# Memory sums of half 0 in 64-row tiles, token sums behind pv(1), and the value copies dealt out anew between ScalarE and VectorE

## The chip, the cores and the metric

The kernel runs on one core of a Trainium2 chip. Its time is the device time of one execution, in microseconds (us); of several runs the median counts. The core's engines run side by side and hand work to each other by semaphores: TensorE (PE in the profile, its weight loads PEld), VectorE (DVE), ScalarE (ACT), GpSimd (POOL) and SyncE (SP), which issues DMAs. TensorE writes its products to PSUM, which is divided into banks; VectorE and ScalarE read them from there and write bfloat16 copies to SBUF, where TensorE can read them.

## The reference

Four stages follow each other, each adding its output to x: A, B, A, B. Stage A is attention over segments of 32 tokens with 8 memory rows that pass from one segment to the next, so the 64 segments of a stage run one after the other. Stage B is a gated mixer over all 2048 tokens; the change doesn't touch it.

```python
def _A_ref(x, mem0, Wq, Wk, Wv, Wo, seg_len):      # x (1, 2048, 512), mem0 (1, 8, 512), Wq/Wk/Wv (512, 32, 128)
    mask = (idx[:, None] < M) | (idx[:, None] >= idx[None, :])
    mem = mem0
    for s in range(n_seg):                          # 64 segments
        h = concatenate([mem, xs], axis=1)          # 8 + 32 rows
        q, k, v = einsum('btd,dhe->bhte', h, Wq), ..., ...
        scores = where(mask, einsum('bhqe,bhke->bhqk', q, k) * scale, -1e9)
        p = softmax(scores, axis=-1)
        o = einsum('bhqk,bhke->bhqe', p, v)
        o = einsum('bhte,hed->btd', o, Wo)
        mem = o[:, :M, :]
        outs.append(o[:, M:, :])
x = x + _A_ref(_layernorm(x), ...)
x = x + _B_ref(_layernorm(x), ...)
x = x + _A_ref(_layernorm(x), ...)
x = x + _B_ref(_layernorm(x), ...)
```

## The kernel before

`a_block` runs stage A and calls `segment` for each of the 64 segments, 128 in the two stages. The order of TensorE, VectorE and ScalarE is the order in which the source issues their instructions; each engine works off its own list in that order, and the semaphores between them are set by a layer that follows which tile each instruction reads and writes. Accesses of two engines to one PSUM bank are ordered too, unless the source declares that there is no dependency (`tc.declare_no_dep`).

The 32 heads go in two halves of 16, r = 0 and 1. One segment does, in TensorE's order:

- queries and keys, four chunks of 16 products of 512 columns (psQ, psm, psK; `mm_chunk`, line 753). TensorE works here as four column tiles of 32 columns each, so four products run together. ScalarE copies each chunk to rows (line 1078), VectorE transposes it (line 1081).
- `v_mm(0)`: the values of half 0, into psK[:, 1, :], with `scores(0)` (lines 1104 and 1108) among them. ScalarE takes the exponential of the scores into S (`exps`, line 1113), VectorE multiplies it by the mask into E (`close`, line 1116). VectorE copies the values to VA[:, 0] (line 1202).
- `v_mm(1)`: the values of half 1, into the bank psW (called psV in the profile), 16 products in four groups. `scores(1)` stands after the second group, `sums_zero` after the third, and the fourth group comes last. ScalarE copies the values to VA[:, 1] (line 1217).
- a piece of other work (`fill`): products for later blocks, psb or pwB in the profile, four of them at this place.
- `pv(0)`: probabilities times values of half 0 (lines 1153 and 1156). From here to `pv(1)` TensorE works as two row tiles of 64 rows and 128 columns each; the keys of one half lie in 128 partitions, and each 64 of them belong to other heads.
- `sums_tokens`: the softmax denominators of the 32 token queries, by products of E with a matrix of ones (line 1145), into psT; `sums_one`: those of the 8 memory queries of half 1 (line 1136), into free columns of psO[1]; `pv(1)`.
- another `fill`, then the output projection of the memory rows: `wo_pairs` for heads 0 to 15 (px, line 936), `wo_rest` for heads 16 to 31 (line 943). It reads uT, which VectorE makes from psO and Rm (`memory_out`, line 1174).

Rm is the inverse of a memory sum, by a logarithm (line 1170) and an exponential (line 1171) on ScalarE (`inverse`). The memory sums of half 0 are made by `sums_zero` in 32-column tiles: 16 products whose left side is `half`, a constant with ones in 64 of its 128 rows and zeros in the others, so that all 128 rows can be streamed and only one group's heads count (line 1127). They land in columns 224 to 352 of the first scores' bank, psS[:, 0, :].

Of the kernel before, what the change touches and what calls it, by code (L numbers as in the profile page):

```python
# [7 lines left out]
BF16 = mybir.dt.bfloat16  # L8
# [6 lines left out]
P = 128  # L15
# [51 lines left out]
def _consts(ctx, tc, c, b_sp, between):  # L67
    nc = tc.nc
    cp = ctx.enter_context(tc.tile_pool(name="consts", bufs=1))
    bsp = cp.tile([P, 16], F32, name="bsp")  # L70
    tctx = ExitStack()
    tmp = tctx.enter_context(tc.tile_pool(name="consts_tmp", bufs=1))
    maskf = tmp.tile([P, 224], F32, name="maskf")
    nc.gpsimd.memset(maskf[:], 1.0)
    fourth = tmp.tile([P, 4, 32], F32, name="fourth")
    nc.gpsimd.memset(fourth[:], 0.0)
    nc.gpsimd.affine_select(out=fourth[:], in_=fourth[:], compare_op=ALU.not_equal, fill=1.0,
                            base=0, pattern=[[-1, 4], [-4, 32]], channel_multiplier=1)
    own = maskf[:, 160:224].rearrange("p (i q) -> p i q", i=4)
    is_own = tmp.tile([P, 4, 1], F32, name="is_own")  # L80
    nc.vector.tensor_reduce(out=is_own[:], in_=fourth[:], op=ALU.max, axis=mybir.AxisListType.X)
    nc.vector.tensor_copy(own, is_own[:].to_broadcast([P, 4, 16]))
    between()
    for q in range(0, P, 32):
        blk = maskf[q:q + 32, 0:160].rearrange("p (i q) -> p i q", i=4)[:, :, 8:32]
        nc.gpsimd.affine_select(out=blk, in_=blk, compare_op=ALU.is_ge, fill=0.0, base=8,
                                pattern=[[0, 4], [1, 24]], channel_multiplier=-1)
        last = own[q:q + 32, :, 8:16]
        nc.gpsimd.affine_select(out=last, in_=last, compare_op=ALU.is_ge, fill=0.0, base=0,
                                pattern=[[1, 4], [4, 8]], channel_multiplier=-1)  # L90
    maskN = cp.tile([P, 2, 224], BF16, name="maskN")
    nc.vector.memset(maskN[:], 0.0)
    for gs in range(4):
        nc.vector.tensor_copy(maskN[32 * gs:32 * gs + 32, gs % 2, :], maskf[32 * gs:32 * gs + 32, :])
    ones = cp.tile([P, P], BF16, name="ones")
    nc.vector.memset(ones[:], 1.0)
    half = cp.tile([P, 2, 32], BF16, name="half")
    nc.vector.memset(half[:], 0.0)
    for g in range(2):
        nc.vector.memset(half[64 * g:64 * g + 64, g, :], 1.0)  # L100
    bsp_bf = cp.tile([P, 16], BF16, name="bsp_bf")

    def load_bsp():
        nc.vector.memset(bsp_bf[:], 0.0)
        nc.sync.dma_start(bsp_bf[:], b_sp.rearrange("(t p) -> p t", p=P))
        return lambda: nc.vector.tensor_copy(bsp[:], bsp_bf[:])

    c["bsp"], c["load_bsp"] = bsp, load_bsp
    tctx.close()
    c.update(maskN=maskN, ones=ones, half=half)  # L110
    return c


# [504 lines left out]
def cols_rhs(w, j, kt, cg):  # L618
    at = 2048 * (j % 2) + 512 * cg
    return w[j // 2][:, kt, at:at + 512]  # L620
# [88 lines left out]
def a_block(tc, c, rows, front, MV_in, RS_in, MV_out, RS_out, ahead, wo, S, first):  # L709
    nc = tc.nc  # L710
    NSEG = S // SEG
    NB = S // P
    scale = float(DH) ** -0.5
    maskN, ones, half = c["maskN"], c["ones"], c["half"]

    with ExitStack() as ctx:

# [33 lines left out]
        def mm_chunk(ps, lhs, rhs, kts=range(KT)):  # L751

            return [nc.tensor.matmul(ps[32 * cg:32 * cg + 32, :], lhsT=lhs(kt, cg), rhs=rhs(kt, cg), start=(kt == 0), stop=(kt == KT - 1),  # L753
                                     tile_position=(0, 32 * cg)) for kt in kts for cg in range(4)]

        def other_bank(mms, *reads):

            for m in mms:
                for r in reads:
                    tc.declare_no_dep(m.ins, r.ins, reason="another bank of the tile")  # L760
# [300 lines left out]
        def segment(s, fill, spare1, spare2, spare3, tail, loads):  # L1061
# [4 lines left out]
            VA = vsp.tile([P, 2, 4, DH], BF16, name="VA")  # L1066
# [6 lines left out]
            E = segp.tile([P, 2, 2, 224], BF16, name="E", bufs=1)  # L1073
# [9 lines left out]
            def v_mm(r, ps, kts=range(KT)):  # L1083
                return mm_chunk(ps, lambda kt, cg: hA_cur[:, kt, :], lambda kt, cg: cols_rhs(w, 4 + r, kt, cg), kts)

            def ends(q):

                return q.rearrange("p h (b e) -> p h b e", e=8)[:, :, 0:5:4, :]
# [5 lines left out]
            def heads40(q):  # L1094
                return q.rearrange("p (i q) -> p i q", q=40)
# [16 lines left out]
            def exps(r):  # L1112
                return nc.scalar.activation(out=S[:, r], in_=psS[:, r, 0:224], func=ACT.Exp, scale=scale)  # L1113

            def close(r):
                nc.vector.tensor_tensor(out=E[:, r], in0=S[:, r].unsqueeze(1).to_broadcast([P, 2, 224]), in1=maskN[:], op=ALU.mult)

            def e_all(e, lo, hi):

                return e[:, :, 0:160].rearrange("p n (i q) -> p n i q", q=40)[:, :, :, lo:hi]  # L1120

            def e_own(e, b):
                return e[:, :, 160:224].rearrange("p n (i b e) -> p n i b e", i=4, b=2)[:, :, :, b, :]

            def sums_zero(pN):

                return [nc.tensor.matmul(pN[32 * cg:32 * cg + 32, 64 * g:64 * g + 64], lhsT=half[:, g, :], rhs=e_own(E[:, 0], 0) if k else e_all(E[:, 0], 0, 8),
                                         start=False, stop=True, tile_position=(0, 32 * cg), skip_group_check=True)
                        for k in range(2) for g in range(2) for cg in range(4)]

            def sums_one():

                for k in range(2):
                    for g in range(2):
                        e = E[64 * g:64 * g + 64, 1]
                        nc.tensor.matmul(psO[1][:, g, 320:384], lhsT=ones[64 * g:64 * g + 64, :], rhs=e_own(e, 0) if k else e_all(e, 0, 8),
                                         start=(k == 0), stop=True, skip_group_check=True)

            def sums_tokens(ps):

# [7 lines left out]
            def pv(r):  # L1148

                for i in range(4):  # L1150
                    for g in range(2):
                        o = psO[r][:, g, 0:320].rearrange("p (s i q) -> p s i q", s=2, i=4)[:, :, i, :]
                        nc.tensor.matmul(o, lhsT=VA[64 * g:64 * g + 64, r, i, :], rhs=E[64 * g:64 * g + 64, r, :, 40 * i:40 * i + 40],  # L1153
                                         start=(r == 0 and i == 0), stop=True, skip_group_check=True)
                for g in range(2):
                    nc.tensor.matmul(ends(heads40(psO[r][:, g, 0:320])), lhsT=VX[64 * g:64 * g + 64, j4, r, :],
                                     rhs=E[64 * g:64 * g + 64, r, :, 160:224], start=False, stop=True, skip_group_check=True)
# [10 lines left out]
            def inverse(r, src):  # L1168
                rm = Rm[:, r]
                nc.scalar.activation(out=rm, in_=src, func=ACT.Ln)  # L1170
                return lambda: nc.scalar.activation(out=rm, in_=rm, func=ACT.Exp, scale=-1.0)  # L1171
# [19 lines left out]
            psK = attO[0].tile([P, 2, 512], F32, name="psK")  # L1191
# [4 lines left out]
            psS = att.tile([P, 2, 512], F32, name="psS")  # L1196
            scores(0)
            expd = exps(0)
            qk_T(3, r3)
            other_bank(v_mm(0, psK[:, 1, :], (1, 2, 3)), read)  # L1200
            close(0)
            nc.vector.tensor_copy(VA[:, 0].rearrange("p i e -> p (i e)"), psK[:, 1, :])
            if j4 == 0 and tb + 1 < NB and not begin:
                ln_turn(tb + 1)
            if begin:
# [1 line left out]
            psW = accB.tile([P, 512], F32, name="psV")  # L1207
            v_mm(1, psW, (0, 1))
            other_bank(scores(1), expd)
            expd = exps(1)  # L1210
            v_mm(1, psW, (2,))
            pN = psS[:, 0, 224:352]
            other_bank(sums_zero(pN), expd)
            v_mm(1, psW, (3,))
            Rm = segp.tile([P, 2, 2, 64], F32, name="Rm", bufs=1)
            invert = inverse(0, pN.rearrange("p (g q) -> p g q", g=2))
            nc.scalar.copy(VA[:, 1].rearrange("p i e -> p (i e)"), psW[:])
            invert()
            close(1)

            psO = [attO[r].tile([P, 2, 512], F32, name="psO") for r in range(2)]
            if not begin:
                fill()
            pv(0)
            psT = att.tile([P, 2, 512], F32, name="psT")
            sums_tokens(psT)
            sums_one()
            pv(1)
            memory_out(0)
            spare1(E)  # L1230
            if not begin:
# [62 lines left out]
        start = nc.vector if first else nc.gpsimd  # L1294
# [137 lines left out]
        for i in range(H // 2):  # L1432
            for k in range(4):
                h = 2 * i + k % 2
                nc.tensor.matmul(pw[32 * k:32 * k + 32, :], lhsT=ends[k // 2][:, h, :], rhs=wo.head(h).rearrange("p (kt g el) -> p g kt el", kt=4, g=4),
                                 start=(i == 0), stop=(i == H // 2 - 1), tile_position=(0, 32 * k))
# [46 lines left out]
```

## Time and profile before

| | |
|---|---|
| median of 3 runs | 1620.24 us |
| lowest and highest | 1613.57 and 1620.24 us |
| profiled execution, its own time | 1608.14 us |
| its span, first to last instruction | 1606.4 us |
| TensorE busy | 1574.8 us, 98% |
| VectorE busy | 1071.0 us, 67% |
| ScalarE busy | 1052.2 us, 65% |
| GpSimd busy | 305.7 us, 19% |

The page of the profile gives busy time and instructions of each engine, the span in 40 slices, the chain of work that ended last, and the costliest groups of instructions (line, engine, operation, output<-inputs, shapes, count | busy us, mean ns of one | idle time of the engine before them and who ended most of it). Other views list who waited for whom, the instructions in order of time, or the busy time in chosen stretches. A busy share is a mean over stages with different limits; what a change in one stage is worth is read from that stage.

### The profile page before, as it was taken

The numbers are of one execution on the slowest core, as the hardware profiler recorded it, in microseconds if no ns is written. First come the engines' busy times: TensorE is split into PE (matmuls) and PEld (weight loads), VectorE is DVE, ScalarE is ACT, GpSimd is POOL, SyncE is SP. The second block draws the span as 40 slices with busy tenths as digits, with TensorE's granted clock in tenths as the row PEclk, the third lists the DMA queues.
The fourth block names the chain that finished last, engine by engine and source line by source line (L and its number), as shares of the span: only waits on it lengthen the run. The fifth ranks groups of instructions, "written<-read, shape, count | busy, mean of one in ns | idle before, by whom it ended". The sixth has DMA issues, their size and how long they took to land.

```text
span 1606.4 us, 90912 instructions
## 1 busy us (share of the span) xinstructions
PE 1574.8 (98%) x41021; PEld 974.9 (61%) x41046; DVE 1071.0 (67%) x3066; ACT 1052.2 (65%) x2279; POOL 305.7 (19%) x674
## 2 busy tenths in 40 slices
PE   7899999999999999999999999999999999999999
PEld 3566666666666666566656666666666666665565
DVE  4666766677777776784466666666677667768622
ACT  4677777777777777660057777777777777776400
POOL 6211121112211221320021111111122112224000
PEclk9999999999999999999999999999999999999999
DMA  9312211222311332368942212211333123426696
GB/s 363 131 56 44 43 45 44 50 40 82 79 43 40 87 91 57 108 169 177 216 153 46 49 44 49 46 47 47 73 93 73 47 70 95 96 56 176 142 199 158
DMA packets 255773, 149.67 MB, mean 93 GB/s; under 512 B 188504, under 2 KB 231104, under 8 KB 255384
## 3 DMA queue, kind: packets, MB, share of 16 engines
q1 hardware_dynamic: 241464, 97.68, 26.9%
q0 software_dynamic: 13920, 46.18, 8.7%
q8 instruction: 321, 5.26, 1.4%
q14 instruction: 68, 0.56, 0.1%
HBM read 60.21 MB, written 39.55 MB: 62 GB/s over the span
## 4 chain that ended last, share of the span: by engine, by line
PE 92%; DMA 4%; issue 1%; DVE 1%; POOL 1%; ACT 0%; POOLq 0%; SPq 0%; DVEq 0%
PE psQ L753 13%; PE psK L753 13%; PE psb L753 10%; PE pg L401 9%; PE psO L943 7%; PE px L936 7%; PE psm L753 7%; PE psV L753 7%; PE pwB L955 3%; PE psO L1153 3%; PE pz L300 3%; PE py L444 2%; PE psT L1145 2%; PE psS L1104 2%; DMA Wk_sb<-in_A_Wk_dram 1%
## 5 line engine op out<-in xcount | busy, mean ns | idle before, releaser
L753 PEld LDWEIGHTS <-hT 128*32 128x32 bf16 x12288 | 340.2, 96 | 262.4 <-DVE hT L1053 17.6
L753 PE MATMUL psV<-Wv_sb,hT 128*32 128x512 bf16 x2048 | 166.0, 379 | 0.0
L1078 ACT CAST rows<-psQ 128x512 bf16<-128x512 f32 x256 | 145.0, 589 | 23.0 <-PE psQ L753 19.4
L1174 DVE TENSOR_TENSOR uT<-psO,Rm 128x128 bf16<-128x128 f32 x256 | 74.7, 292 | 123.5 <-ACT Rm L1171 122.9
L1081 DVE STREAM_TRANSPOSE QQ<-rows 128x256 f32<-128x256 f32 x256 | 112.3, 439 | 65.1 <-ACT rows L1078 62.7
L1113 ACT ACTIVATE S<-psS 128x224 bf16<-128x224 f32 x256 | 92.2, 360 | 96.2 <-PE psS L1108 96.0
L1081 DVE STREAM_TRANSPOSE KA<-rows 128x256 f32<-128x256 f32 x256 | 113.0, 441 | 62.7 <-ACT rows L1078 60.2
L401 PE MATMUL pg<-z,wspT 128*128 128x344 bf16 x1024 | 154.3, 309 | 0.0
L753 PE MATMUL psK<-Wv_sb,hT 128*32 128x512 bf16 x2048 | 152.8, 378 | 0.0
L1177 DVE TENSOR_TENSOR uT<-psO,Rt 128x384 bf16<-128x384 f32 x256 | 139.7, 546 | 17.3 <-ACT Rt L1256 16.0
L1256 ACT ACTIVATE Rt<-Rt 128x512 f32<-128x512 f32 x256 | 147.3, 622 | 4.0
L943 PE MATMUL psO<-Wo_high,uT 128*32 128x128 bf16 x8192 | 140.7, 219 | 4.5 <-issue 2.9
L936 PE MATMUL px<-Wo,uT 128*32 128x256 bf16 x3840 | 133.9, 273 | 2.0 <-issue 1.9
L753 PE MATMUL psQ<-Wq_sb,hT 128*32 128x512 bf16 x2048 | 135.7, 379 | 0.0
L753 PE MATMUL psQ<-Wk_sb,hT 128*32 128x512 bf16 x2048 | 135.7, 379 | 0.0
L753 PE MATMUL psm<-Wq_sb,hT 128*32 128x512 bf16 x2048 | 135.6, 379 | 0.0
L753 PE MATMUL psK<-Wk_sb,hT 128*32 128x512 bf16 x2048 | 135.6, 379 | 0.0
L401 PEld LDWEIGHTS <-wspT 128*128 128x128 bf16 x1024 | 100.1, 98 | 53.4 <-issue 0.4
L1253 ACT ACTIVATE Rt<-psT 128x1024 f32<-128x1024 f32 x127 | 130.2, 1025 | 3.1
L943 PEld LDWEIGHTS <-uT 128*32 128x32 bf16 x8192 | 123.2, 97 | 14.7 <-issue 6.8
L936 PEld LDWEIGHTS <-uT 128*32 128x32 bf16 x4096 | 104.3, 97 | 26.1 <-issue 3.4
L1035 POOL COPY KX<-old 128x128 bf16<-128x128 bf16 x128 | 64.9, 535 | 264.3 <-PE psS L1108 146.0
(224 smaller groups left out, 2888.9 us busy)
## 6 DMA issues: line engine op xcount, KB each, us to landing
o_d<-o_sb SPq DMA_DIRECT2D x126, 64.0 KB
vb_d<-front SPq DMA_DIRECT2D x31, 256.0 KB
VX<-vb_d SPq DMA_DIRECT2D x124, 64.0 KB
ln_x<-xd SPq DMA_DIRECT2D x26, 256.0 KB
y_o<-o_d POOLq DMA_DIRECT2D x22, 256.0 KB, 3.3
xd<-y_o POOLq DMA_DIRECT2D x22, 256.0 KB, 3.0
Wq_sb<-in_A_Wq_dram POOLq DMA_DIRECT2D x8, 512.0 KB, 7.1
Wk_sb<-in_A_Wk_dram POOLq DMA_DIRECT2D x8, 512.0 KB, 9.4
```

The lines of the kernel that those rows point to most:

```text
L401: nc.tensor.matmul(pg[t][:, k, 0:344], lhsT=wsp[t][:, st, :], rhs=z(st, 344 * k, 344 * k + 344), start=(st == 0), stop=(st == NT - 1))
L753: return [nc.tensor.matmul(ps[32 * cg:32 * cg + 32, :], lhsT=lhs(kt, cg), rhs=rhs(kt, cg), start=(kt == 0), stop=(kt == KT - 1), tile_posi ...
L936: nc.tensor.matmul(px[at:at + 32, 0:256], lhsT=lhs[:, h, :], rhs=wo_rhs(h, slice(k + 2, None, -2) if h % 2 else slice(k, None, 2)), start= ...
L943: nc.tensor.matmul(pw[32 * cg:32 * cg + 32, :], lhsT=lhs[:, h, :], rhs=wo_rhs(h, cg), start=False, stop=(h == H - 1), tile_position=(0, 32 ...
L1035: eng.tensor_copy(KX[r][:].rearrange("p g (k i) -> p i g k", i=4), bs["KTB"][:, r].rearrange("p (i g) k -> p i g k", i=4)[:, :, :, 8 * j4: ...
L1078: return r, mms, copy(r[:].rearrange("p (n el two) -> p n el two", n=8, two=2), ps.rearrange("p (n two el) -> p n el two", n=8, two=2))
L1081: nc.vector.transpose(out=(QQ[:, j % 2, :, 0:32] if j < 2 else KA[:, j % 2]).bitcast(F32).rearrange("p n q one -> p n (q one)"), in_=r[:]. ...
L1113: return nc.scalar.activation(out=S[:, r], in_=psS[:, r, 0:224], func=ACT.Exp, scale=scale)
L1174: nc.vector.tensor_tensor(out=hview(uT_cur[:], r, 24, 32), in0=oview(r, 0, 8), in1=Rm[:, r].rearrange("p g (n q) -> p g n q", q=8), op=ALU ...
L1177: nc.vector.tensor_tensor(out=hview(uT_nxt[:], r, 0, 24), in0=oview(r, 8, 32), in1=rview(r, 0, 24), op=ALU.mult)
L1253: nc.scalar.activation(out=Rt[:], in_=psT[:], func=ACT.Ln)
L1256: nc.scalar.activation(out=rt, in_=rt, func=ACT.Exp, scale=-1.0)
```

## The change

- `sums_zero`, its constant `half` and `sums_one` go. `sums_memory(r, ps, begun)` does the memory sums of either half in the way of `sums_one`: four products with ones in 64-row tiles.
- Half 0's sums move from inside `v_mm(1)` to just ahead of `pv(0)`, and land in columns 224 to 288 of both banks of psS, where the scores' products have begun the accumulation. Half 1's sums go ahead of `pv(1)`, and `sums_tokens` goes behind it.
- VA[:, 0] is copied by ScalarE in place of VectorE.
- VA[:, 1] is copied in two halves of 256 columns, the first by ScalarE, the second by VectorE. On VectorE the copy stands behind the close of half 1, `close(1)`, which moves ahead of it in the source.
- Logarithm and exponential of half 0's inverse move behind these copies on ScalarE, one right after the other.

```diff
-            def sums_zero(pN):
-
-                return [nc.tensor.matmul(pN[32 * cg:32 * cg + 32, 64 * g:64 * g + 64], lhsT=half[:, g, :], rhs=e_own(E[:, 0], 0) if k else e_all(E[:, 0], 0, 8),
-                                         start=False, stop=True, tile_position=(0, 32 * cg), skip_group_check=True)
-                        for k in range(2) for g in range(2) for cg in range(4)]
-
-            def sums_one():
+            def sums_memory(r, ps, begun):
 
                 for k in range(2):
                     for g in range(2):
-                        e = E[64 * g:64 * g + 64, 1]
-                        nc.tensor.matmul(psO[1][:, g, 320:384], lhsT=ones[64 * g:64 * g + 64, :], rhs=e_own(e, 0) if k else e_all(e, 0, 8),
-                                         start=(k == 0), stop=True, skip_group_check=True)
+                        e = E[64 * g:64 * g + 64, r]
+                        nc.tensor.matmul(ps[:, g, :], lhsT=ones[64 * g:64 * g + 64, :], rhs=e_own(e, 0) if k else e_all(e, 0, 8),
+                                         start=(k == 0 and not begun), stop=True, skip_group_check=True)
...
-            nc.vector.tensor_copy(VA[:, 0].rearrange("p i e -> p (i e)"), psK[:, 1, :])
+            nc.scalar.copy(VA[:, 0].rearrange("p i e -> p (i e)"), psK[:, 1, :])
...
             expd = exps(1)
-            v_mm(1, psW, (2,))
-            pN = psS[:, 0, 224:352]
-            other_bank(sums_zero(pN), expd)
-            v_mm(1, psW, (3,))
+            v_mm(1, psW, (2, 3))
+            close(1)
+            for k, copy in enumerate((nc.scalar.copy, nc.vector.tensor_copy)):
+                copy(VA[:, 1, 2 * k:2 * k + 2].rearrange("p i e -> p (i e)"), psW[:, 256 * k:256 * k + 256])
             Rm = segp.tile([P, 2, 2, 64], F32, name="Rm", bufs=1)
-            invert = inverse(0, pN.rearrange("p (g q) -> p g q", g=2))
-            nc.scalar.copy(VA[:, 1].rearrange("p i e -> p (i e)"), psW[:])
-            invert()
-            close(1)
 
             psO = [attO[r].tile([P, 2, 512], F32, name="psO") for r in range(2)]
             if not begin:
                 fill()
+            sums_memory(0, psS[:, :, 224:288], True)
             pv(0)
+            inverse(0, psS[:, :, 224:288])()
+            sums_memory(1, psO[1][:, :, 320:384], False)
+            pv(1)
             psT = att.tile([P, 2, 512], F32, name="psT")
             sums_tokens(psT)
-            sums_one()
-            pv(1)
             memory_out(0)
```

More of the change, by code (lines that the diff above doesn't have):

```diff
@@ L96, in _consts @@
     nc.vector.memset(ones[:], 1.0)
[L97 to L100, printed above, removed]
     bsp_bf = cp.tile([P, 16], BF16, name="bsp_bf")
@@ L109, in _consts @@
     tctx.close()
-    c.update(maskN=maskN, ones=ones, half=half)
+    c.update(maskN=maskN, ones=ones)
     return c
@@ L713, in a_block @@
     scale = float(DH) ** -0.5
-    maskN, ones, half = c["maskN"], c["ones"], c["half"]
+    maskN, ones = c["maskN"], c["ones"]
     with ExitStack() as ctx:
```

## The prediction

> **What bounds the kernel now.** I read the page first, then the list of waits, then the order of time inside one segment of stage A, then the groups by shape for durations.
>
> ```profile
> span 1606.4 us, 90912 instructions
> PE 1574.8 (98%) x41021; PEld 974.9 (61%) x41046; DVE 1071.0 (67%) x3066; ACT 1052.2 (65%) x2279; POOL 305.7 (19%) x674
> PEclk9999999999999999999999999999999999999999
> PE 92%; DMA 4%; issue 1%; DVE 1%; POOL 1%; ACT 0%; POOLq 0%; SPq 0%; DVEq 0%
> ```
>
> TensorE is busy for 98% of the span at a full granted clock and makes up 92% of the chain that ended last. VectorE and ScalarE have a third of the span free. The stage to read is the segment, run 128 times:
>
> ```profile
> 253.24:263.27 10.03, 10.03 (x312) 6.09 (x308) 7.12 (x23) 7.91 (x20) 1.44 (x4) 1.00 0.24 62
> ```
>
> This row of the windows view (stretch, its length, then busy time of PE, PEld, DVE, ACT, POOL) is one segment from its psV projection to the next: 10.03 us, TensorE busy in all of it. So a wait that the change brings to TensorE finds no idle time in the segment to vanish in, and time saved on TensorE counts only if what follows is ready earlier too. The list of TensorE's waits agrees. Each row names who waited for whom, the us in total, the times and the longest; of 128 segments only a few wait at all for a transposed key or for E:
>
> ```profile
> PE psS L1104 <- DVE KA L1081: 1.6, 2, 1.2
> PE psT L1145 <- DVE E L1116: 1.5, 1, 1.5
> ```
>
> Now the order of time (start, length, engine, line, what). A matmul row's length includes a tail after the next group has begun, so for TensorE I go by differences of starts.
>
> ```profile
> 251.39 1.04 PE L753 MATMUL psK<-Wk_sb,hT 128*32 128x512 bf16 x16
> 252.47 0.59 ACT L1078 CAST rows<-psK 128x512 bf16<-128x512 f32 x1 [0.28 <-PE psK L753]
> 252.60 0.82 PE L753 MATMUL psK<-Wv_sb,hT 128*32 128x512 bf16 x12
> 252.96 0.36 ACT L1113 ACTIVATE S<-psS 128x224 bf16<-128x224 f32 x1
> 253.46 0.35 DVE L1116 TENSOR_TENSOR E<-S,maskN 128x448 bf16<-128x448 bf16 x1
> 253.73 0.68 DVE L1202 CAST VA<-psK 128x512 bf16<-128x512 f32 x1
> 254.03 0.29 PE L1127 MATMUL psS<-E,half 128*32 128x64 bf16 x16
> 254.07 0.36 ACT L1113 ACTIVATE S<-psS 128x224 bf16<-128x224 f32 x1 [0.75 <-PE psS L1108]
> 254.14 0.39 PE L753 MATMUL psV<-Wv_sb,hT 128*32 128x512 bf16 x4
> 254.35 0.39 PE L753 MATMUL psb<-Wq_sb,hB 128*32 128x512 bf16 x4
> 254.38 0.28 ACT L1170 ACTIVATE Rm<-psS 128x128 f32<-128x128 f32 x1
> 254.46 0.39 DVE L1116 TENSOR_TENSOR E<-S,maskN 128x448 bf16<-128x448 bf16 x1
> 254.58 0.59 ACT L1217 CAST VA<-psV 128x512 bf16<-128x512 f32 x1
> 254.68 0.32 PE L1153 MATMUL psO<-E,VA 64*128 64x80 bf16 x8
> 254.91 0.45 PE L1145 MATMUL psT<-E,ones 64*128 64x512 bf16 x4
> 255.06 0.31 ACT L1171 ACTIVATE Rm<-Rm 128x128 f32<-128x128 f32 x1
> 255.19 0.22 PE L1136 MATMUL psO<-E,ones 64*128 64x64 bf16 x4
> 255.25 0.31 PE L1153 MATMUL psO<-E,VA 64*128 64x80 bf16 x8
> 255.39 0.22 PE L1156 MATMUL psO<-E,VX 64*128 64x128 bf16 x2
> 255.54 0.61 PE L753 MATMUL psb<-Wq_sb,hB 128*32 128x512 bf16 x8
> ```
>
> The reader is to see two tight covers. Second E (closed by VectorE, 254.46 + 0.39 = 254.85) is first read by the token sums at 254.91: TensorE reaches them just as E is there. And the second values' copy on ScalarE (254.58 + 0.59 = 255.17) is first read by pv(1) at 255.25; in between TensorE does token sums (254.91 to 255.19, 0.28) and the sums of half 1 (0.06). These 0.34 us are what hides that copy.
>
> **The change, part by part.**
>
> *Half 0's sums.* The 16 products with half, 254.03 to 254.14, 0.11 us, go; four products with ones in 64 rows come in front of pv(0). The same shape is the row at 255.19, 0.06 us until 255.25. TensorE saves 0.05 us a segment, 128 × 0.05 = 6 us, if what follows lets it. The three constants' memsets at the start are nothing against the span.
>
> Where it stands now: the psV projection is done 0.11 us earlier (254.14 + 0.39 − 0.11 = 254.42), the psb products start at 254.24 and, with today's 0.33 us from there to the first product in 64 rows (254.35 to 254.68), half 0's sums start at 254.57, pv(0) at 254.63. From pv(0) to the next group take today's 0.23 (254.68 to 254.91): 254.86 at the latest. There stand half 1's sums, and they read second E, which still closes at 254.85 and is seen by TensorE 0.06 later, at 254.91: second scores, exponential and close are not moved by the change. So the 0.05 us won ahead of it are spent waiting for E. From 254.91 the rest is the same work in another order: 0.06 + 0.14 (pv(1) up to its VX products, 255.25 to 255.39) + 0.15 (those and the turn to 32-column tiles, 255.39 to 255.54) + 0.28 = 0.63, and the psb products start at 255.54 as before. **At its best the change gives nothing.**
>
> *The token sums behind pv(1).* They no longer lie between second E and pv(1). pv(1) may start at 254.91 + 0.06 = 254.97, its third pair of heads (half of 0.14 on) at 255.04. The second values must be there 0.2 us sooner than now.
>
> *The second values' copy, by halves.* In the built program VectorE's half waits for one semaphore, ScalarE's, at the count that ScalarE's own half raises; TensorE waits for ScalarE before the first load of pv(1) and for VectorE before the fifth, that is the third pair. So the halves run one after the other. Durations by width:
>
> ```profile
> L1217 ACT CAST VA<-psV 128x512 bf16<-128x512 f32 x128 | 75.0, 586 | 0.0
> L1113 ACT ACTIVATE S<-psS 128x224 bf16<-128x224 f32 x256 | 92.2, 360 | 96.2 <-PE psS L1108 96.0
> L1170 ACT ACTIVATE Rm<-psS 128x128 f32<-128x128 f32 x128 | 35.6, 278 | 0.0
> L1202 DVE CAST VA<-psK 128x512 bf16<-128x512 f32 x128 | 87.0, 680 | 0.1
> L1044 DVE COPY cross<-px 64x128 f32<-64x128 f32 x128 | 36.3, 284 | 43.2 <-PE px L936 42.2
> ```
>
> 256 columns are not in the trace. ScalarE: between 360 ns (224) and 586 (512), on the line through 278 (128) and 586: 278 + 128 × 0.80 = 0.38 us. VectorE: between 284 (128) and 680 (512): 284 + 128 × 1.03 = 0.42 us. Hand-overs: TensorE to ScalarE 0.04 (psK ends 251.39 + 1.04 = 252.43, its copy starts 252.47), up to 0.09 at second scores; I take 0.05. ScalarE to VectorE 0.03 (exponential ends 254.43, close starts 254.46). VectorE to TensorE 0.06 (254.85 to 254.91).
>
> ScalarE's half: 254.42 + 0.05 = 254.47 (the engine is free from 254.38 on, where its next instruction starts today), ends 254.85. VectorE's half: 254.88, after second E's close anyway, ends 255.30. TensorE's third pair: 255.36 in place of 255.04, a stall of 0.32. Then 0.07 + 0.15 + 0.28 = 0.50, and the psb products start at **255.86 against 255.54: 0.32 us a segment later**.
>
> What queues behind the stalled load: the other half of pv(1), token sums, eight psb products, all of Wo's. Nobody else is late by more than TensorE. Behind VectorE's half waits the first uT product, which needs Rm 0: its sums end near 254.8 (begun 254.57, and the row at 255.19 is 0.22 long), logarithm and exponential (0.28 + 0.31, 0.03 handed over) bring it to about 255.5, and Wo's first half stands behind the stall and eight psb products. Rm 1's logarithm follows the end of pv(1) as today (255.39 + 0.22 = 255.61), and the token sums, 0.28, are added between pv(1) and Wo, so Wo's second half waits for it less than today.
>
> *First values on ScalarE.* psK's values end at 252.60 + 0.82 = 253.42, the copy starts at 253.47 (first exponential ended 253.32) and holds ScalarE for 0.48 us (254.58 to 255.06, the start of the next), until 253.95. Second exponential starts at 254.07 anyway: the idle 0.75 us in its row are the cover. Cost nothing; without that cover second E, and all behind it, would be late by the same amount. pv(0) needs these values at 254.63, long after.
>
> *The rule for and against.* The Trainium skill, "TensorEngine Tiling (Array Packing)", section PSUM Bottleneck, advises to evacuate PSUM with both ScalarE and VectorE. The Trainium skill, "PSUM — Partial Sum Buffer", section "PSUM bank collisions raise a hardware error", says that the two must not touch one bank in the same partitions at once, reads against reads included. Both halves here read one bank of psV, so by the second rule the order one after the other is needed, and by the first alone the sum would be that of rival B.
>
> **Sum.** 128 × 0.32 = 41 us. On the profiled execution, 1608.14 us, that is 1649. The runs shown have their median at 1620.24, 12.1 us above it, and I add the same: **1661 us**, 2.5% slower.
>
> Bounds: were the two half copies as short as the 128-column rows (0.28 each), the stall would be 0.24 shorter, +0.08 a segment, 10 us; as long as the full ones (0.59 and 0.68), it would be 0.47 longer, +0.79, 101 us. Below nothing it can't go, since second E holds the end at +0. I take values near the 128-column side because both engines' rows grow evenly with width and the 224-column row (0.36 on ScalarE) fits the line (0.28 + 96 × 0.80 = 0.36); that leaves some 0.06 us either way, 8 us.
>
> **Rivals.**
>
> B, 0.08: ScalarE's half does not hold up VectorE's. Then VectorE's starts straight after close, at 254.77 (first E ended 253.81, the copy behind it started 253.73, 0.08 sooner), ends 255.19, seen 255.25; psb at 255.75, +0.21, 27 us: 1647. For it: separate columns. Against: the wait in the built program.
>
> C, 0.05, the other side: not slower. The second values are there when pv(1) wants its third pair, at 255.04. That needs VectorE's half finished by 254.98, while VectorE closes second E until 254.85. For it: VectorE and ScalarE have idle time in plenty. Against: even begun at 254.77, as in B, the half copy would have to take 0.21 us or less, below the 284 ns of 128 columns; from there on it decides. Then psb starts at 255.54 again, +0: 1620. A gain would need second E earlier too, which nothing here brings: 0.02 for faster, 6 us at most.
>
> D, 0.08: pv(1) waits as a whole for both halves, as would be if TensorE took the fifth load's wait before its first. Then all of pv(1) stands behind 255.36: 0.07 more, +0.39, 50 us: 1670. Against: two separate waits.
>
> Left, 0.07: a size off by more than I allow, slower all the same.
>
> **How the numbers follow.** The forecast has 0.70, with own range 1653 to 1669. B and D lie on either side and are taken in, and the runs shown differ by 7 us among themselves: range 1642 to 1676. A measurement of this kernel can tell about 0.5%, 8 us, from no change. Slower: the forecast, B, D and the rest, 0.93. Same: C without its gain, 0.05. Faster 0.02.
>
> **What would show it.** Right: in the profile after, TensorE's weight loads of pv wait on VectorE's VA copy, about 0.3 us in each segment, some 40 us in all; the VectorE half starts 0.03 after ScalarE's ends; segments take 10.35 us; half 0's sums take 0.06. Second exponential still starts 0.82 us after the psV projection does. Wrong: VectorE's half beside ScalarE's, no gap inside pv(1), or a second exponential that is late behind the first values' copy.

## The result and the profile after

| | before | changed |
|---|---|---|
| median | 1616.90 us (1612.16 to 1620.24, 4 runs) | 1636.58 us (1634.55 to 1638.16, 4 runs) |
| ratio, 95% interval | | 1.013 (1.0107 to 1.0153) |
| profiled execution, span | 1606.4 us | 1636.4 us |

The changed kernel is slower by 1.3%, some 20 us. The forecast had 41 us more and 1661 us, with a range from 1642. In a second series the ratio was 1.0148 (1.0133 to 1.0163), 24 us. The sign and the stall were forecast, the size came out at half.

The page of the changed kernel's profile: span, busy time of the engines, chain that ended last.

```profile
span 1636.4 us, 87964 instructions
PE 1591.9 (97%) x39485; PEld 966.4 (59%) x39510; DVE 1047.6 (64%) x3063; ACT 1127.4 (69%) x2407; POOL 306.0 (19%) x674
PE 47%; DVE 5%; ACT 4%; DMA 1%; issue 1%; POOL 0%; DVEq 0%; POOLq 0%; SPq 0%
```

TensorE has 3072 instructions fewer (matmuls and weight loads), ScalarE 75 us more work. ScalarE and VectorE, at 0% and 1% of the chain before, now make up 4% and 5%. The order of time in the same segment as before (start, length, engine, line, what), with the psV projection's start at 257.40 in place of 253.24:

```profile
257.40 0.60 PE L749 MATMUL psV<-Wv_sb,hT 128*32 128x512 bf16 x8
257.62 0.59 ACT L1192 CAST VA<-psK 128x512 bf16<-128x512 f32 x1
258.22 0.36 ACT L1109 ACTIVATE S<-psS 128x224 bf16<-128x224 f32 x1
258.40 0.39 PE L749 MATMUL psb<-Wq_sb,hB 128*32 128x512 bf16 x4
258.61 0.39 DVE L1112 TENSOR_TENSOR E<-S,maskN 128x448 bf16<-128x448 bf16 x1 [0.65 <-ACT S L1109]
258.62 0.37 ACT L1204 CAST VA<-psV 128x256 bf16<-128x256 f32 x1
258.72 0.23 PE L1126 MATMUL psS<-E,ones 64*128 64x64 bf16 x4
258.79 0.31 PE L1143 MATMUL psO<-E,VA 64*128 64x80 bf16 x8
259.02 0.42 DVE L1204 CAST VA<-psV 128x256 bf16<-128x256 f32 x1
259.06 0.23 PE L1126 MATMUL psO<-E,ones 64*128 64x64 bf16 x4
259.11 0.64 PE L1143 MATMUL psO<-E,VA 64*128 64x80 bf16 x8
259.50 0.11 PEld L1143 LDWEIGHTS <-VA 64*128 64x128 bf16 x4 [0.28 <-DVE VA L1204]
259.64 0.43 PE L1135 MATMUL psT<-E,ones 64*128 64x512 bf16 x4
260.01 0.40 PE L749 MATMUL psb<-Wq_sb,hB 128*32 128x512 bf16 x4
```

The reader is to see ScalarE's half (258.62 + 0.37 = 258.99), VectorE's behind it (259.02 to 259.44), and TensorE's weight load of the third pair of pv(1) at 259.50, released by VectorE's VA. From the psV projection to the next psb products pass 2.61 us, before 2.30: 0.31 more. The list of waits (who, for whom, us in total, times, longest) has the row in all 128 segments:

```profile
PEld L1143 <- DVE VA L1204: 34.4, 128, 0.3
```

So the stall is there as forecast. But 128 times 0.31 are 40 us, and only 30 lie between the two profiles, 20 to 24 between the medians. To see where the rest went I take the distance from each segment's psV projection to the next one's, for segments 2 to 125 without those next to stage B: 60 long ones and 61 short ones (those with less other work in them). "Regular" is the distance that a fifth of them stay below; "beyond" is the sum over all 121 of what they take longer than that.

```
profile                span     regular long, short   beyond
before                 1606.4   10.030   9.669        13.4 us
before, second         1616.0   10.033   9.671        20.5 us
changed                1636.4   10.345   9.981         4.6 us
changed, second        1635.6   10.342   9.979         4.2 us
```

The regular segment got 0.31 us longer, 39 us over some 126 of them, and irregular waits of 13 to 20 us shrank to 4. They also make the kernel before vary: its two profiles differ by 9.6 us, 7.1 of it in this column. The experiments ask whether the stall is made as forecast, and why the irregular waits shrank: because a stall takes them up (theory S), or because TensorE has 24 instructions a segment fewer (theory N).

### The profile page after: what moved, and what is told of

The parts are those of the page before. It is cut to its first block, busy times and chain, and to the rows that moved or that the text cites. A ratio compares the mean times of both kernels' runs of the same rounds, so it can differ in the third digit from the quotient of the medians.

```text
span 1636.4 us, 87964 instructions
## 1 busy us (share of the span) xinstructions
PE 1591.9 (97%) x39485; PEld 966.4 (59%) x39510; DVE 1047.6 (64%) x3063; ACT 1127.4 (69%) x2407; POOL 306.0 (19%) x674
## 4 chain that ended last, share of the span: by engine, by line
PE 47%; DVE 5%; ACT 4%; DMA 1%; issue 1%; POOL 0%; DVEq 0%; POOLq 0%; SPq 0%
PE pg L397 9%; PE psQ L749 7%; PE psK L749 7%; PE psb L749 4%; PE psO L939 3%; PE px L932 3%; PE psm L749 3%; PE pz L296 3%; PE py L440 2%; ACT VA L1192 2%; DVE VA L1204 2%; DVE E L1112 1%; PE pwB L951 1%; ACT S L1109 1%; PE psT L1135 1%
## 5 line engine op out<-in xcount | busy, mean ns | idle before, releaser
L749 PEld LDWEIGHTS <-hT 128*32 128x32 bf16 x12288 | 327.0, 96 | 262.2 <-DVE hT L1049 17.0
L749 PE MATMUL psV<-Wv_sb,hT 128*32 128x512 bf16 x2048 | 150.5, 378 | 0.0
L1112 DVE TENSOR_TENSOR E<-S,maskN 128x448 bf16<-128x448 bf16 x256 | 96.2, 376 | 83.9 <-ACT S L1109 83.8
L939 PE MATMUL psO<-Wo_high,uT 128*32 128x128 bf16 x8192 | 137.1, 219 | 2.1 <-DMA Wo_high<-in_A_Wo_dram 1.4
L939 PEld LDWEIGHTS <-uT 128*32 128x32 bf16 x8192 | 127.4, 97 | 3.7 <-issue 2.1
L932 PEld LDWEIGHTS <-uT 128*32 128x32 bf16 x4096 | 109.4, 97 | 25.1 <-issue 2.3
L1143 PE MATMUL psO<-E,VA 64*128 64x80 bf16 x2048 | 102.7, 199 | 17.5 <-DVE VA L1204 0.8
```

What stands on the lines that cost most here:

```text
L932: nc.tensor.matmul(px[at:at + 32, 0:256], lhsT=lhs[:, h, :], rhs=wo_rhs(h, slice(k + 2, None, -2) if h % 2 else slice(k, None, 2)), start= ...
L939: nc.tensor.matmul(pw[32 * cg:32 * cg + 32, :], lhsT=lhs[:, h, :], rhs=wo_rhs(h, cg), start=False, stop=(h == H - 1), tile_position=(0, 32 ...
```

## The experiments

Ratios are against the kernel before, run beside them.

**Token sums last, alone** (kernel before):

```diff
-            psT = att.tile([P, 2, 512], F32, name="psT")
-            sums_tokens(psT)
             sums_one()
             pv(1)
+            psT = att.tile([P, 2, 512], F32, name="psT")
+            sums_tokens(psT)
```

> The kernel before with one part of the change alone: the token sums stand behind pv(1). Sums of half 0 and both copies as before. Segment theory: the second values are seen by TensorE at 1.98 us after the psV projection begins (copy ends 1.925, 0.05 handed over), pv(1) would be reached at 1.72, so each segment gets 0.26 us longer: 10.03 becomes 10.29, 128 x 0.26 = 33 us. Theory S (a stall in each segment takes up the irregular waits of TensorE, some 12 us of them in the profile of before): those shrink to 4 us as in the changed kernel, so +20 to +25 us over the median of before. Theory N (they shrank in the changed kernel because 24 instructions a segment are gone): all instructions are still there, so they stay, +33 us.

Measured: 1634.81 us, ratio 1.0138 (1.0113 to 1.0163), 22 us more; regular 10.287 and 9.923, beyond 8.5 us. The order of time shows the wait ahead of pv(1), between the sums (L1136) and the first product (L1153):

```profile
258.19 0.58 ACT L1217 CAST VA<-psV 128x512 bf16<-128x512 f32 x1
258.52 0.23 PE L1136 MATMUL psO<-E,ones 64*128 64x64 bf16 x4
258.83 0.32 PE L1153 MATMUL psO<-E,VA 64*128 64x80 bf16 x8
```

The sums take 0.06; pv(1) starts 0.31 after them, 0.06 behind the end of the copy at 258.77. The segment grew by 0.26, as expected, so the token sums were the cover of this copy. With every instruction still there, the irregular waits fell, but not to 4 us: the 22 us are theory S's, and theory N alone, at +33, falls.

**The copies alone** (kernel before):

```diff
-            nc.vector.tensor_copy(VA[:, 0]..., psK[:, 1, :])
+            nc.scalar.copy(VA[:, 0]..., psK[:, 1, :])
...
-            nc.scalar.copy(VA[:, 1]..., psW[:])
-            invert()
             close(1)
+            for k, copy in enumerate((nc.scalar.copy, nc.vector.tensor_copy)):
+                copy(VA[:, 1, 2 * k:2 * k + 2]..., psW[:, 256 * k:256 * k + 256])
+            invert()
```

> The kernel before with the copies of the change alone: first values on ScalarE, second values by halves, all sums as before. Segment theory: ScalarE's half runs from 1.34 to 1.71 us after the psV projection begins, VectorE's from 1.75 to 2.17, TensorE sees it at 2.23 in place of 2.07 for the third pair of pv(1): +0.15 us a segment, 20 us. Theory S: less 8 to 12 us of irregular waits, +8 to +12. Theory N: +20. If the split helped, as it would with both halves side by side, the segment would stay at 10.03 us.

Measured: ratio 1.0074 (1.005 to 1.0098), 12 us more; regular 10.187 and 9.826, beyond 10.9 us. The 0.16 a segment is the expected 0.15: the split costs time even with the token sums in place.

**Second values copied whole** (changed kernel):

```diff
-            for k, copy in enumerate((nc.scalar.copy, nc.vector.tensor_copy)):
-                copy(VA[:, 1, 2 * k:2 * k + 2]..., psW[:, 256 * k:256 * k + 256])
+            nc.scalar.copy(VA[:, 1]..., psW[:])
```

> The changed kernel with the second values copied whole by ScalarE, everything else as changed. Segment theory: the copy runs from 1.22 to 1.81 us after the psV projection begins, pv(1) starts at 1.86 in place of 1.72: +0.14 us a segment against before (18 us), 0.18 less than the changed kernel (23 us less). With the irregular waits small as in the changed kernel, +3 to +10 us over the median of before. If the split were worth its while, this would be slower than the changed kernel.

Measured: ratio 1.0048 (1.0031 to 1.0065), 8 us more; regular 10.168 and 9.861, beyond 4.3 us. Without the split the long segment is 0.18 shorter than the changed kernel's, as expected. The short ones gained only 0.12: there fewer products stand ahead of Wo, and it waits for the first uT, a row that the changed kernel has once, with 0.3 us:

```profile
PEld L932 <- DVE uT L1164: 10.9, 63, 0.5
```

**384 columns on ScalarE, 128 on VectorE** (changed kernel):

```diff
-            for k, copy in enumerate((nc.scalar.copy, nc.vector.tensor_copy)):
-                copy(VA[:, 1, 2 * k:2 * k + 2]..., psW[:, 256 * k:256 * k + 256])
+            for copy, lo, hi in ((nc.scalar.copy, 0, 3), (nc.vector.tensor_copy, 3, 4)):
+                copy(VA[:, 1, lo:hi]..., psW[:, 128 * lo:128 * hi])
```

> The changed kernel with the second values split 384 to 128 columns between ScalarE and VectorE in place of 256 to 256. Segment theory, one after the other: ScalarE from 1.22 to 1.70 us after the psV projection begins, VectorE from 1.74 to 2.02, seen at 2.08 for the fourth pair of pv(1): +0.25 us a segment against before, 0.07 less than the changed kernel, 9 us less. If VectorE's part began with the close of E alone, it would end at about 1.81 and the segment would be 0.2 us shorter than the changed kernel's.

Measured: ratio 1.0089 (1.0067 to 1.0112), 14 us more, 7 to 10 less than the changed kernel; regular 10.280 and 9.920, beyond 3.4 us. VectorE's part starts 0.03 behind ScalarE's end:

```profile
257.50 0.39 DVE L1112 TENSOR_TENSOR E<-S,maskN 128x448 bf16<-128x448 bf16 x1 [0.65 <-ACT S L1109]
257.51 0.48 ACT L1204 CAST VA<-psV 128x384 bf16<-128x384 f32 x1
258.02 0.29 DVE L1204 CAST VA<-psV 128x128 bf16<-128x128 f32 x1
```

257.51 + 0.48 = 257.99, while second E was closed at 257.89 already. In the halves of the changed kernel, too, VectorE begins 0.03 after ScalarE's end (258.99, 259.02), so the parts do run one after the other.

**Token sums first** (changed kernel):

```diff
+            psT = att.tile([P, 2, 512], F32, name="psT")
+            sums_tokens(psT)
             sums_memory(1, psO[1][:, :, 320:384], False)
             pv(1)
-            psT = att.tile([P, 2, 512], F32, name="psT")
-            sums_tokens(psT)
```

> The changed kernel with the token sums in their old place, ahead of half 1's sums and pv(1). If the place of the token sums alone made the stall, they would cover the copies again and only 0.03 us a segment were left, +4 us over before. Segment theory: the token sums write the buffer that half 0's sums stand in (psT and psS share it), so they wait for the logarithm of half 0, which ends 1.87 us after the psV projection begins, seen at 1.92 in place of 1.66: +0.26 us a segment, 33 us, less what irregular waits shrink, +20 to +25.

Measured: ratio 1.0094 (1.0073 to 1.0115), 15 us more; regular 10.287 and 9.930, beyond 4.6 us. The token sums wait for the logarithm of half 0:

```profile
257.37 0.37 ACT L1204 CAST VA<-psV 128x256 bf16<-128x256 f32 x1
257.74 0.28 ACT L1160 ACTIVATE Rm<-psS 128x128 f32<-128x128 f32 x1
258.07 0.45 PE L1135 MATMUL psT<-E,ones 64*128 64x512 bf16 x4 [0.17 <-ACT Rm L1160]
```

257.74 + 0.28 = 258.02, and they start 0.05 later. So the two moves of the change hang together: with half 0's sums made late, in the buffer that the token sums take over, the token sums can't go early, and the cover can't be had back by putting them there.

**VX products first, ScalarE alone** (changed kernel; 384 columns, then 128):

```diff
-            for k, copy in enumerate((nc.scalar.copy, nc.vector.tensor_copy)):
-                copy(VA[:, 1, 2 * k:2 * k + 2]..., psW[:, 256 * k:256 * k + 256])
+            for lo, hi in ((0, 3), (3, 4)):
+                nc.scalar.copy(VA[:, 1, lo:hi]..., psW[:, 128 * lo:128 * hi])
...
             def pv(r):
+                if r == 1:
+                    pv_x(r)
                 for i in range(4):
...
+                if r == 0:
+                    pv_x(r)
```

> The changed kernel with the second values copied by ScalarE alone, 384 columns and then 128, and with the products of pv(1) that need no copied values (those with VX) ahead of the others. Segment theory: the first piece is there at 1.76 us after the psV projection begins, the last at 1.93, where TensorE would ask for it at 1.88: +0.05 us a segment, 6 us. With irregular waits of 4 us in place of 12 or more, 2 to 9 us below the median of before; if those waits stay, 6 us above it.

A miss: ratio 1.0093 (1.007 to 1.0117), 15 us more; regular 10.212 and 9.922, beyond 5.8 us. I had left out of the sum what stands behind the two pieces on ScalarE:

```profile
257.63 0.65 ACT L1211 CAST VA<-psV 128x384 bf16<-128x384 f32 x2
258.16 0.30 ACT L1167 ACTIVATE Rm<-psS 128x128 f32<-128x128 f32 x1
258.18 0.36 PE L1151 MATMUL psO<-E,VA 64*128 64x80 bf16 x8
258.51 0.45 PE L1135 MATMUL psT<-E,ones 64*128 64x512 bf16 x4
```

pv(1) runs without a gap, but the logarithm begins only at 258.16 and ends at 258.46, and the token sums, which take over its buffer, start 0.05 after that; further on Wo waits for the first uT in 123 segments, 22.4 us in all. This was to be the version that beats both kernels, and it doesn't.

**Half 1's sums four times over** (changed kernel):

```diff
-            sums_memory(1, psO[1][:, :, 320:384], False)
+            for _ in range(4):
+                sums_memory(1, psO[1][:, :, 320:384], False)
```

> The changed kernel with half 1's memory sums done four times over, 24 instructions more a segment, as many as the change removed, and 0.17 us of TensorE inside its stall of 0.32. Segment theory: the segment stays at 10.34 us. Theory S (stall takes up irregular waits): same as the changed kernel within 0.3%. Theory N (fewer instructions): irregular waits come back, 8 us or more slower than the changed kernel.

Measured: ratio 1.0195 (1.0174 to 1.0216), 31 us more; regular 10.345 and 9.982, the changed kernel's to within 0.001, beyond 9.3 us. The same stall with the old number of instructions is 7 to 10 us slower than the changed kernel: instructions that cost no time in the regular segment cost it in irregular waits. Theory S alone falls; theory N's price is met.

**Instructions left out of the kernel before:** 16 a segment (half of `sums_zero`), then 24 (also the products with VX).

```diff
-                        for k in range(2) for g in range(2) for cg in range(4)]
+                        for k in range(1) for g in range(2) for cg in range(4)]
...
-                for g in range(2):
-                    nc.tensor.matmul(ends(heads40(psO[r][:, g, 0:320])), lhsT=VX[64 * g:64 * g + 64, j4, r, :],
-                                     rhs=E[64 * g:64 * g + 64, r, :, 160:224], start=False, stop=True, skip_group_check=True)
```

> The kernel before without half of the products of half 0's memory sums (those of the own columns, 8 of 16): 16 instructions and 0.06 us of TensorE a segment are left out. Segment theory: E of half 1 holds what follows, the segment stays at 10.03 us and at 9.67 in the short ones, so no regular gain. Theory N: irregular waits of TensorE shrink, the median falls by 4 to 10 us. Neither theory: no change within 0.3%.

> The kernel before without half of the products of half 0's memory sums and without the products with VX in both halves: 24 instructions a segment are left out, as many as the change removed, and no stall is added. Segment theory: the products with VX of half 1 stand behind second E, so the segment gets 0.05 us shorter, 7 us in all; those of half 0 stand ahead of it and win nothing. Theory N by count: irregular waits fall to 3 to 5 us in the profile, the median falls by 12 to 20 us. If the number of instructions doesn't matter at this size: irregular waits of 9 to 13 us in the profile, the median falls by 5 to 9 us.

Measured: 0.9969 (0.9956 to 0.9981) with 16 fewer, 5 us less, regular 10.031 and 9.669; 0.9921 (0.9904 to 0.9937) with 24 fewer, 13 us less, regular 9.974 and 9.611, which accounts for 7 of them. That leaves 5 to 6 us for the number of instructions in either. The profile's column doesn't show it cleanly: beyond 17.3 us with 16 fewer, within what the two profiles of before span, and 8.7 with 24 fewer, between the two expectations. So fewer instructions help without a stall, but do not bring the irregular waits to 4 us by themselves.

**Both kernels once more**, for a second profile and a narrower ratio; their numbers stand in the first section.

> The kernel before once more, for a second profile: regular segments of 10.03 and 9.67 us, and irregular waits of TensorE of 8 to 14 us if those of the first profile were no accident.

> The changed kernel once more beside the others, for a second profile and a narrower ratio: 1.010 to 1.016 times the kernel before, regular segments of 10.34 and 9.98 us, irregular waits of 3 to 6 us in the profile.

Both came as expected, but for the irregular waits of the kernel before, 20.5 us, above the 14 that I allowed.

## Why the prediction was right in mechanism and wrong in size

- *No gain from half 0's sums.* Right: they take 0.07 us (258.72 to 258.79), and half 1's sums start at 259.06 behind second E's close (258.61 + 0.39 = 259.00), as E allows.
- *First values on ScalarE cost nothing.* Right: second exponential starts 0.82 us after the psV projection, 0.83 before.
- *The halves one after the other.* Right, with the sizes of the sum: 0.37 us on ScalarE (0.38 taken), 0.42 on VectorE (0.42), 0.03 and 0.06 handed over. Rivals B and C fall by these rows. The Trainium skill, "PSUM — Partial Sum Buffer", section "PSUM bank collisions raise a hardware error", says that two engines must not read one bank in the same partitions at once; the program keeps to that, 0.03 us from the one's end to the other's start, and no run here let both read at once. The Trainium skill, "TensorEngine Tiling (Array Packing)", section PSUM Bottleneck, recommends both engines; that did not pay here, where both read one bank: split in halves, the second values made the long segment 0.18 us longer than copied whole by ScalarE. Rival D falls by the order of time, where pv(1) starts at 259.11 and stops halfway.
- *0.32 us a segment.* Right: 0.31 in the regular segment, 39 to 40 us in all. Of the parts, token sums last alone make 0.26 and the copies alone 0.16; together less than their sum, since both make pv(1) wait for the same values.
- *"So a wait that the change brings to TensorE finds no idle time in the segment to vanish in".* This is the step that failed. I read one segment without a gap and a list of waits by semaphores, and took all segments for like it. The kernel before has irregular waits of 13 and 20 us in its two profiles, most of it TensorE idle with nothing to wait for. Rows of this stood in the very list that I quoted from, `PE psO L943 <- issue: 2.9, 8, 0.9` three places above the first one shown, and I did not add them up.
- *"I add the same", 12.1 us from the profiled execution to the median.* This went wrong with it. The profiled execution of before, 1608.14 us, lies below all of its other runs, and 1620.24, the median of three, near the top of them: the 7 to 18 runs beside the experiments have medians of 1612.01 to 1613.89. The changed kernel's runs keep within 4 us, its profiled one at 1638.16. The scatter that I carried over is largely in the waits that shrank. Of the 24 us between 1661 and 1636.58, some 11 come from the stall (41 forecast, 30 between the profiles) and some 14 from this term, which was 12.1 and came out at -1.6.

The forecast's 41 us less what was measured, 20 to 24, leaves 17 to 21. By the regular segments and the ratios beside them, the kernels divide thus (126 segments; time measured less 63 times both regular differences; "stall" is the mean of these two):

```
                                  stall    measured less regular
as many instructions as before    0.16     12 - 20 = -8 us      copies alone
                                  0.26     22 - 32 = -10 us     token sums last
                                  0.31     31 - 40 = -9 us      sums four times over
24 fewer                          none     -13 + 7 = -6 us      products left out
                                  0.17      8 - 21 = -13 us     second values copied whole
                                  0.22     15 - 27 = -12 us     VX products first
                                  0.25     14 - 32 = -18 us     384 to 128
                                  0.26     15 - 33 = -18 us     token sums first
                                  0.31     24 - 40 = -16 us     changed kernel
```

A stall takes back 8 to 10 us whichever way it is made, 24 instructions fewer 6 without a stall and 7 to 10 with the same one, and both together 12 to 18. That is the missing part: now and then TensorE runs out of instructions in the kernel before (the last section shows where), and either a pause in each segment or a shorter program makes that rarer.

## What to carry to other kernels

A copy split between two engines pays only if the second part is not held up. Here it was: the parts read one bank and were ordered, and the second engine was still busy with the operand that the same products need, so the split cost more than it saved. Before cover is moved away from behind a copy, work out what holds the moved work in its new place and whether it can ever go back: token sums and half 0's sums share a buffer. And before a stall is priced one for one on a busy TensorE, add up the waits that no semaphore ends over all segments and over more than one profile, since a regular stall can replace part of them.

## What the runs showed of the hardware

The irregular waits have "issue" in the profile: the engine waited for nothing that it shows. In the kernel before one of them looks like this in the order of TensorE alone:

```profile
127.99 0.78 PE L943 MATMUL psO<-Wo_high,uT 128*32 128x128 bf16 x41
129.65 0.29 PE L943 MATMUL psO<-Wo_high,uT 128*32 128x128 bf16 x7 [0.89 <-issue]
```

Wo's second half stops in its middle, with all operands there. The rows of waits for Wo's weight loads, which have hardly any regular part, in the kernel before, then its second profile, then the changed kernel, then the one with sums four times over:

```profile
PEld L943 <- issue: 6.8, 12, 1.8
PEld L936 <- issue: 3.4, 4, 1.7
```

```profile
PEld L943 <- issue: 9.1, 21, 1.1
PEld L936 <- issue: 4.2, 6, 2.2
```

```profile
PEld L932 <- issue: 2.3, 2, 1.3
PEld L939 <- issue: 2.1, 2, 1.8
```

```profile
PEld L939 <- issue: 4.4, 7, 1.8
PEld L932 <- issue: 2.9, 4, 1.2
```

The page's row of the queue that carries instructions, before and after (packets, MB, share of 16 engines):

```profile
q8 instruction: 321, 5.26, 1.4%
```

```profile
q8 instruction: 309, 5.06, 1.3%
```

5.26 MB over TensorE's 41021 matmuls and 41046 weight loads are 64 bytes each, and the 12 packets fewer, of 16 KB, over the 3072 instructions fewer are 64 bytes again: this queue brings TensorE its program, 256 instructions to a packet, 2.4 packets a segment. A gap is here, in the 121 segments, more than 0.33 us between the starts of two matmuls, without the lines that have one in nearly every segment. With a packet about every 4 us some 17% of them would end 1.0 to 1.7 us after one had landed by chance:

```
profile                      gaps   1.0 to 1.7 us after a packet   at one place of 256   these add up to   beyond
before                        17               14                          13                8.5 us         13.4
before, second                30               25                          25               13.9 us         20.5
sums four times over          13               11                          11                6.1 us          9.3
changed                        6                2                           2                0.7 us          4.6
changed, second                6                2                           2                0.8 us          4.2
```

For the column "at one place" TensorE's matmuls, weight loads and entries for semaphores are counted from the start of the program. In the first three rows most gaps stand at the same place of each 256 instructions, the length of a packet: at 188 or 189 in the first stage A and at 166 or 167 in the second. (25 matmuls have no record in these traces, which shifts the count; with the copies alone none is missing, and 10 of 14 gaps stand at 192 or 193 in both stages.) The gap shown above is one of them, at 189, 1.6 us after a packet had landed.

TensorE passes this place some 280 times in the segments of each profile. In these five, the next matmul never starts there less than 1.2 us after the latest packet has landed. The gaps of the kernel before all end 1.2 to 1.6 us after it, while half of all passages come more than 2.4 and 2.1 us after it in its two profiles, 2.5 with the sums four times over, 2.8 in the changed kernel. So these gaps stand where the count of one packet's instructions comes round, and only where a packet has just landed: TensorE waits for its next instructions. Most of what "beyond" lost from the kernel before to the changed one is such gaps.

The Trainium skill, "Runtime: NRT & Kernel Launch", section "Instruction fetch mechanics", has programs fetched in blocks of 16 KiB and calls the cost of crossing a block mostly hidden. The block size agrees with the trace, and most crossings show no gap here either; but the 13 and 25 that do cost some 8 and 14 us. That late instructions are the cause rests on these places and times and on the runs with more and fewer instructions. No run changed the fetching itself, and why a packet comes late in some segments and not in others stays open.
